# A linear-attention layer's products as 512 and 128 columns, keys one block ahead of values, and a closing stage that begins with two denominators

## The chip, the cores and the metric

The kernel runs on one core of one Trainium2 chip. The core has a matrix engine (TensorE, "PE"; its weight loads are listed apart as "PEld"), a vector engine (DVE), a scalar engine for activations (ACT), a general engine (POOL) and a queue engine (SP) that mostly issues transfers. Each engine runs its own list of instructions in order and waits on semaphores set by the others. The metric is the device time of the whole program in microseconds; the time of a kernel is the median of its runs.

## The reference

Two kinds of residual layer alternate, A, B, A, B, over 2048 tokens of width 640:

```
x = x + A(layernorm(x))     # twice, alternating with
x = x + B(layernorm(x))
```

A is attention with a recurrent memory: 64 segments of 32 tokens, each with 8 memory rows that are the first outputs of the segment before, 32 heads of 192. It is a chain of 64 dependent steps and takes most of the time. The change does not touch it. B is linear attention with a softmax feature map, 32 heads of 20:

```
q, k, v = split(x @ wqkv)                        # 32 heads x 20 each
pq, pk  = q @ w_phi[h], k @ w_phi[h]             # per head, 20 x 20
phi(p)  = [softmax(p), softmax(-p)]              # over the head's 20
kv      = sum over tokens of phi(pk)^T v         # per head, 40 x 20
z       = sum over tokens of phi(pk)
out     = (phi(pq) @ kv) / (phi(pq) @ z + 1e-6)
return out @ wo
```

No token's output can be formed before kv and z have been summed over all 2048 tokens, so the layer has two stages.

## The kernel before

The layers A run by a schedule that is written out by hand. A layer B is written as plain loops; a scheduler (Tile) orders its instructions on each engine by their dependences and by when buffers come free, so the order in the code is not always the order on the engine. The layers B run at about 1563 to 1863 us (layer 1) and 3420 to 3679 us (layer 3, the last). The end of the attention layer before it is computed inside B (`multiply`, lines 1192 to 1206): its products already go as 512 and 128 columns on one stationary block, into a kv bank and a side bank, and ACT and DVE evict them.

All products of B accumulate in PSUM, which has eight banks: three hold kv and z through the first stage (`kvp`), three rotate as the general banks (`bank()`, pool `pp`), two as the side banks (`side_bank()`, pool `ptp`). An instruction that wants a bank waits until the one that had it has been read out.

The layer works in four groups of 512 tokens, each of four blocks of 128. `norm_rows` adds the attention's output to the rows (POOL, line 360) and normalises them; `turn_rows` transposes them. The first stage of a group:

- `keys_values` (line 403), block by block. Keys (line 410): two halves of 320 columns, each of five matmuls over the input's 640 rows, into a bank each; ACT takes exp(p) and exp(-p) from each bank (line 413). DVE sums the exponentials of each head (line 416) and inverts the sums (line 418); POOL copies them beside the values (line 421). Values (line 425): again two halves; DVE multiplies each by the inverse sums (line 429). Then ten kv products of up to 126 columns (line 435). `w_phi` has been multiplied into the weights earlier (`fuse`).
- `query_norms` of the group before (line 451): the sums of the query exponentials (line 457), their logs on ACT (line 349), the difference on DVE (line 460), `split_exp` (lines 342 to 344: two exps on ACT, a subtraction on DVE), and then for six chunks of heads a spreading product (line 465) and a multiply on DVE (line 466).
- `queries` (line 446): six chunks of 120 (the last 40) rows by 512 tokens, with two exps each on ACT (line 449).

After the four groups kv and z are masked into block-diagonal form (`kvm`, `zm`, lines 512 to 520), and the closing stage runs: for a group, `denominators` (line 527: twelve matmuls of 512, then log and `split_exp`), `attention` (six chunks: two numerator matmuls, line 538, a spreading product of the inverse denominators, line 541, its copy on ACT, line 543, a multiply on DVE, line 544), and `output_rows` (per block two halves of 320 columns, line 555, the residual add on DVE, line 557, the store by POOL's queue, line 559; in layer 1 also the next layer's row norm and its store, line 563). The closing loop in full:

```
hl = denominators(0)
for g in range(NG):
    oT = attention(g, hl)
    if g + 1 < NG:
        hl = denominators(g + 1)
    if g == 0:
        query_norms(waiting)
    output_rows(g, oT)
```

So the first attention waits for one denominator, its log, two exponentials and a subtraction; later denominators are issued behind the attention before them. The norms of the last group (`waiting`) come behind the first attention. Denominators, norm sums and spreading products use the side banks.

Of the kernel before, what the change touches and what calls it, by code (L numbers as in the profile page):

```python
# [8 lines left out]
P = 128  # L9
# [106 lines left out]
class Kernel:  # L116
# [133 lines left out]
    def layer_B(self, x_dram, at_dram, xout_dram, xnext_dram, li, bp, post):  # L250
# [9 lines left out]
        HB2 = H // 2  # L260
        W2 = D // 2
# [13 lines left out]
        lgs, hls = self.views(take(4096), 2048, 2, F32), self.views(take(2048), 1024, 2)  # L275
# [19 lines left out]
        with tc.tile_pool(name=f"B{li}_kv", bufs=1, space=bass.MemoryType.PSUM, reuse_waits="tile") as kvp, \  # L295
                tc.tile_pool(name=f"B{li}_pt", bufs=2, space=bass.MemoryType.PSUM, reuse_waits="tile") as ptp, \
                tc.tile_pool(name=f"B{li}_ps", bufs=3, space=bass.MemoryType.PSUM, reuse_waits="tile") as pp:
# [104 lines left out]

            def keys_values(g, xnT):
                for b in range(4 * g, 4 * g + 4):
                    q = P * (b - 4 * g)
                    ek = eks.next().rearrange("p (s d) -> p s d", s=2)
                    for u in range(2):
                        ps = bank("ps_pk")
                        for k in range(KC):
                            nc.tensor.matmul(ps[:, 0:W2], lhsT=xnT[:, k, q:q + P],  # L410
                                             rhs=wqkv[:, k, D + W2 * u:D + W2 * u + W2], start=(k == 0), stop=(k == KC - 1))
                        for sg in range(2):
                            nc.scalar.activation(out=ek[:, sg, W2 * u:W2 * u + W2], in_=ps[:, 0:W2], func=ACT.Exp,
                                                 scale=1.0 - 2.0 * sg)
                    sk = bp.tile([P, 2 * H], F32, name="sk", tag="sk")
                    nc.vector.reduce_sum(out=sk[:], in_=ek[:, :, :].rearrange("p s (h f) -> p (s h) f", f=DH), axis=AX.X)
                    rk = bp.tile([P, 2, H], F32, name="rk", tag="rk")
                    nc.vector.reciprocal(out=rk[:, :, :].rearrange("p s h -> p (s h)"), in_=sk[:])

                    vr = vrs.next().rearrange("p (s h f) -> p s h f", s=2, h=H)  # L420
                    nc.gpsimd.tensor_copy(out=vr[:, :, :, DH], in_=rk[:])
                    for u in range(2):
                        ps = bank("ps_v")
                        for k in range(KC):
                            nc.tensor.matmul(ps[:, 0:W2], lhsT=xnT[:, k, q:q + P],
                                             rhs=wqkv[:, k, 2 * D + W2 * u:2 * D + W2 * u + W2], start=(k == 0),
                                             stop=(k == KC - 1))
                        for sg in range(2):
                            nc.vector.tensor_tensor(out=vr[:, sg, HB2 * u:HB2 * u + HB2, 0:DH],
                                                    in0=ps[:, 0:W2].rearrange("p (h f) -> p h f", f=DH),  # L430
                                                    in1=bcast_last(rk[:, sg, HB2 * u:HB2 * u + HB2], DH), op=ALU.mult)
                    for sg in range(2):
                        for c in range(NC_):
                            nh = sizes[c] // DH
                            nc.tensor.matmul(kv_out(sg, c), lhsT=ek[:, sg, CH * c:CH * c + sizes[c]],
                                             rhs=vr[:, sg, HC * c:HC * c + nh, :].rearrange("p h f -> p (h f)"),
                                             start=(b == 0 and (NC_ * sg + c) % 4 == 0), stop=(b == NB - 1),
                                             skip_group_check=True)

# [11 lines left out]
            def query_norms(g):  # L451
# [10 lines left out]
                for c in range(NC_):  # L462
                    mc = sizes[c]
                    pe = side_bank("ps_e")
# [28 lines left out]
            for g in range(NG):  # L493
# [10 lines left out]
                if waiting is not None:  # L504
                    query_norms(waiting)
# [16 lines left out]
            def denominators(g):  # L522
                tk = slice(512 * g, 512 * g + 512)
                ps = side_bank("ps_den")
# [6 lines left out]
            def attention(g, hl):  # L531
                tk = slice(512 * g, 512 * g + 512)
                oT = oTs.next().rearrange("p (c t) -> p c t", c=NC_)
                for c in range(NC_):
# [5 lines left out]
                    pe = side_bank("ps_e")  # L540
# [6 lines left out]
            def output_rows(g, oT):  # L547
                for b in range(4 * g, 4 * g + 4):
# [3 lines left out]
                    for u in range(2):  # L552
                        ps = bank("ps_wo")
                        for c in range(NC_):
                            nc.tensor.matmul(ps[:, 0:W2], lhsT=oT[0:sizes[c], c, q:q + P],
                                             rhs=wo[0:sizes[c], c, W2 * u:W2 * u + W2], start=(c == 0), stop=(c == NC_ - 1))
# [685 lines left out]
```

## Time and profile before

| | |
|---|---|
| time, median of 3 runs | 3674.0 us (3673.94 to 3683.37) |
| the profiled execution: its own time | 3680.76 us |
| the profiled execution: span | 3678.8 us |
| PE busy | 3527.4 us (96%) |
| DVE, ACT, POOL busy | 2339.3, 2044.9, 1653.2 us |
| granted clock, mean | 0.98 |
| a steady group of 512 tokens, layer 1 | 31.7 us |
| start of the closing stage, layer 1 and 3 | 24.6 and 21.5 us |
| the rest of it, layer 1 and 3 | 79.1 and 60.1 us |

The span runs from the first instruction to the last one of the profiled execution; its own time lies 2.0 us above it. "PEclk" is the clock that TensorE was granted, where 1.00 is full speed, and a matmul of the same shape takes twice as long at 0.50. A row of the timeline or of a group names the engine, the line of the kernel, the operation, and its tiles (output, then inputs, with partitions by elements); in brackets stands the idle time of the engine just ahead of it and what ended that.

### The profile page before, as it was taken

The numbers are of one execution on the slowest core, as the hardware profiler recorded it, in microseconds if no ns is written. First come the engines' busy times: TensorE is split into PE (matmuls) and PEld (weight loads), VectorE is DVE, ScalarE is ACT, GpSimd is POOL, SyncE is SP. The second block draws the span as 40 slices with busy tenths as digits, with TensorE's granted clock in tenths as the row PEclk, the third lists the DMA queues.
The fourth block names the chain that finished last, engine by engine and source line by source line (L and its number), as shares of the span: only waits on it lengthen the run. The fifth ranks groups of instructions, "written<-read, shape, count | busy, mean of one in ns | idle before, by whom it ended". The sixth has DMA issues, their size and how long they took to land.

```text
span 3678.8 us, 168780 instructions
## 1 busy us (share of the span) xinstructions
PE 3527.4 (96%) x70978; PEld 2301.1 (63%) x71271; DVE 2339.3 (64%) x6292; ACT 2044.9 (56%) x5233; POOL 1653.2 (45%) x4309
## 2 busy tenths in 40 slices
PE   9999999999999999999999899999999999999998
PEld 7766666666666666655367666666666666666553
DVE  5566666666666666556433566666666666666464
ACT  3356666666666656546332566666666666666462
POOL 3445555555555555430342455555555555555300
PEclk9999999999999999989799999999999999999998
DMA  8988888888888878840377887888888888888500
GB/s 296 342 296 293 277 279 292 285 277 294 283 274 291 290 266 289 304 140 1 135 255 203 292 286 273 292 290 279 295 283 278 289 288 274 289 293 299 155 1 29
DMA packets 531731, 933.33 MB, mean 254 GB/s; under 512 B 141066, under 2 KB 298394, under 8 KB 530970
## 3 DMA queue, kind: packets, MB, share of 16 engines
q1 hardware_dynamic: 428794, 818.87, 63.6%
q0 software_dynamic: 68512, 90.42, 8.3%
q10 hardware_dynamic: 33664, 13.24, 1.4%
q8 instruction: 557, 9.13, 1.0%
q14 instruction: 204, 1.67, 0.1%
HBM read 852.43 MB, written 73.73 MB: 252 GB/s over the span
## 4 chain that ended last, share of the span: by engine, by line
PE 37%; DMA 6%; DVE 4%; ACT 3%; issue 3%; PEld 2%; POOL 1%; SPq 0%; POOLq 0%; ACTq 0%; DVEq 0%
PE ps_qk L948 10%; PE ps_w L1024 4%; PE ps_v L948 4%; PE ps_o L998 2%; PE ps_s L990 2%; DMA arena<-wo_rows 2%; PE ps_pq L446 1%; PE ps_s L1056 1%; PEld L839 1%; DVE hT L904 1%; PE ps_s L985 1%; DMA kqb<-arena 1%; PE ps_idle L1031 1%; DMA arena<-in_A_Wv_dram 1%; PE ps_pk L410 1%
## 5 line engine op out<-in xcount | busy, mean ns | idle before, releaser
L948 PEld LDWEIGHTS <-hT 128*32 128x32 bf16 x30720 | 738.5, 96 | 433.5 <-DVE hT L1168 29.3
L948 PE MATMUL ps_qk<-arena,hT 128*32 128x384 bf16 x20480 | 996.9, 327 | 12.7 <-DMA arena<-in_A_Wk_dram 3.3
L958 ACT ACTIVATE raw<-ps_qk 128x384 bf16<-128x384 f32 x1024 | 503.1, 491 | 379.1 <-PE ps_s L1056 243.8
L1024 PE MATMUL ps_w<-arena,OT 128*32 128x160 bf16 x24576 | 540.9, 234 | 27.5 <-issue 14.9
L931 POOL DMA_DIRECT2D Vp<-vb x512 | 258.8, 505 | 653.9 <-PE ps_o L998 450.6
L948 PE MATMUL ps_v<-arena,hT 128*32 128x384 bf16 x10240 | 537.4, 330 | 5.6 <-DMA arena<-in_A_Wv_dram 5.5
L1024 PEld LDWEIGHTS <-OT 128*32 128x32 bf16 x24576 | 434.9, 97 | 120.3 <-issue 41.7
L963 DVE STREAM_TRANSPOSE KT<-raw 128x384 bf16<-128x384 bf16 x512 | 296.0, 578 | 196.6 <-ACT raw L958 192.6
L966 DVE STREAM_TRANSPOSE QT<-raw 128x256 bf16<-128x256 bf16 x512 | 227.9, 445 | 238.8 <-ACT raw L958 196.1
L919 POOL DMA_DIRECT2D kqb<-kqb x512 | 291.1, 569 | 174.6 <-POOL KT L927 147.9
L979 DVE CAST Vp<-ps_v 64x384 bf16<-64x384 f32 x512 | 286.0, 559 | 95.4 <-ACT Vp L977 80.5
L1017 POOL DMA_DIRECT2D otb<-otb x512 | 282.8, 552 | 110.1 <-DVE otb L1013 96.3
L977 ACT ACTIVATE Vp<-ps_v 64x384 bf16<-64x384 f32 x512 | 246.3, 481 | 150.7 <-PE ps_v L948 113.2
L1004 DVE CAST OT<-ps_o 128x192 bf16<-128x192 f32 x512 | 183.2, 358 | 214.8 <-PE ps_o L998 196.6
L1063 DVE TENSOR_TENSOR E<-E,ps_s 80x320 bf16<-80x320 bf16 x512 | 247.6, 484 | 73.7 <-ACT ps_s L1062 69.7
L1042 ACT ACTIVATE E<-ps_s 80x320 bf16<-80x320 f32 x512 | 221.9, 433 | 124.2 <-PE ps_s L990 95.7
L998 PEld LDWEIGHTS <-Vp 80*128 80x128 bf16 x4096 | 183.7, 99 | 159.4 <-issue 124.6
L998 PE MATMUL ps_o<-E,Vp 80*128 80x80 bf16 x4096 | 234.5, 202 | 24.4 <-DMA Vp<-vb 5.0
L990 PE MATMUL ps_s<-QT,KT 128*80 128x80 bf16 (+1 forms) x3072 | 233.6, 213 | 21.5 <-DVE KT L963 13.2
L1003 ACT ACTIVATE OT<-ps_o 128x192 bf16<-128x192 f32 x512 | 167.8, 328 | 147.6 <-PE ps_o L998 147.3
L912 ACT ACTIVATE Vp<-ps_w 32x160 bf16<-32x160 f32 x512 | 150.7, 294 | 167.4 <-DVE wt L1167 152.5
L990 PEld LDWEIGHTS <-KT 128*80 128x80 bf16 x3072 | 195.0, 119 | 70.7 <-issue 60.9
(157 smaller groups left out, 5329.9 us busy)
## 6 DMA issues: line engine op xcount, KB each, us to landing
arena<-wo_rows SPq DMA_DIRECT2D x792, 320.0 KB, 6.8
arena<-in_A_Wq_dram SPq DMA_DIRECT2D x427, 384.0 KB, 4.7
arena<-in_A_Wv_dram SPq DMA_DIRECT2D x427, 384.0 KB, 6.3
arena<-in_A_Wk_dram SPq DMA_DIRECT2D x768, 192.0 KB, 4.7
kqb<-kqb POOLq DMA_DIRECT2D x512, 48.0 KB, 5.1
arena<-in_A_Wk_dram SPq DMA_DIRECT2D x43, 384.0 KB, 7.1
vb<-arena POOLq DMA_DIRECT2D x128, 112.0 KB, 6.0
Vp<-vb POOLq DMA_DIRECT2D x512, 28.0 KB, 4.8
```

Source lines behind the costliest of these rows:

```text
L919: nc.gpsimd.dma_start(out=kqb[:], in_=self.kqb_d[s, :, r, :])
L931: nc.gpsimd.dma_start(out=Vs[n % 2][64:80, :], in_=self.vb_d[s, r].rearrange("g t f -> (g t) f"))
L948: nc.tensor.matmul(o[32 * g:32 * g + 32, 0:384], lhsT=hT[:, b, :], rhs=rhs, start=(i == 0), stop=(i == KC - 1), tile_position=(0, 32 * g), ...
L958: nc.scalar.activation(out=raw[:], in_=ps[:, 0:384], func=ACT.Copy)
L963: nc.vector.transpose(out=KT[:, :, 0:64], in_=raw[:, :].rearrange("p (c j) -> p c j", j=64))
L977: nc.scalar.activation(out=o, in_=i, func=ACT.Copy)
L979: nc.vector.tensor_copy(out=o, in_=i)
L990: nc.tensor.matmul(S[0:80, c0:c0 + 80 * (q1 - q0)], lhsT=KT[:, 3 * x + i, :], rhs=QT[:, x, q0:q1, :], start=False, stop=(x == 1 and i == 2 ...
L998: nc.tensor.matmul(O[x][:, 80 * i:80 * i + 80], lhsT=Vs[n % 2][0:80, 448 * x + k:448 * x + k + 128], rhs=E[0:80, 160 * x + 80 * e:160 * x ...
L1017: nc.gpsimd.dma_start(out=self.otb_d[s, :, 96 * r:96 * r + 96], in_=otb[:, :, :].rearrange("p c t -> p (c t)"))
L1024: nc.tensor.matmul(W[32 * g:32 * g + 32, 0:160], lhsT=OT[:, c, q:q + 32], rhs=w[:, 640 * i + 160 * g:640 * i + 160 * g + 160], start=(firs ...
L1063: nc.vector.tensor_tensor(out=E[0:80, 0:320], in0=E[0:80, 0:320], in1=rc, op=ALU.mult)
```

## The change

A helper, `pair`, issues for each of n input chunks a matmul of the first 512 columns and one of the last 128 on the same stationary block, into two general banks at once (500 and 140 for values, so that each part holds whole heads). Keys, values and output rows use it in place of two loops over halves of 320. ACT's exps and DVE's multiplies and adds are split in the same way. Keys of a block are issued before the values of the block before it. The banks are shared out as four general and one side bank. Norms and denominators are told which kind of bank to take; attention's spreading product takes a general one. The closing stage begins with the denominators of groups 0 and 1; the norms of the last group still follow the first attention, and each later group issues the denominator of the next. In the last layer the stores go by SP's queue.

```diff
-        lgs, hls = self.views(take(4096), 2048, 2, F32), self.views(take(2048), 1024, 2)
+        lgs, hls = self.views(take(4096), 2048, 2, F32), self.views(take(3072), 1024, 3)
...
-                tc.tile_pool(name=f"B{li}_pt", bufs=2, space=bass.MemoryType.PSUM, reuse_waits="tile") as ptp, \
-                tc.tile_pool(name=f"B{li}_ps", bufs=3, space=bass.MemoryType.PSUM, reuse_waits="tile") as pp:
+                tc.tile_pool(name=f"B{li}_pt", bufs=1, space=bass.MemoryType.PSUM, reuse_waits="tile") as ptp, \
+                tc.tile_pool(name=f"B{li}_ps", bufs=4, space=bass.MemoryType.PSUM, reuse_waits="tile") as pp:
...
+            def pair(name, split, n, lhsT, rhs):
+
+                ps = [bank(name) for _ in range(2)]
+                for k in range(n):
+                    for i, (lo, hi) in enumerate(((0, split), (split, D))):
+                        nc.tensor.matmul(ps[i][:, 0:hi - lo], lhsT=lhsT(k), rhs=rhs(k, lo, hi), start=(k == 0), stop=(k == n - 1))
+                return (ps[0], 0, split), (ps[1], split, D)
+
             def keys_values(g, xnT):
-                for b in range(4 * g, 4 * g + 4):
+                VS = DH * (512 // DH)
+
+                def tokens(b):
                     q = P * (b - 4 * g)
+                    return lambda k: xnT[:, k, q:q + P]
+
+                def keys(b):
                     ek = eks.next().rearrange("p (s d) -> p s d", s=2)
-                    for u in range(2):
-                        ps = bank("ps_pk")
-                        for k in range(KC):
-                            nc.tensor.matmul(ps[:, 0:W2], lhsT=xnT[:, k, q:q + P],
-                                             rhs=wqkv[:, k, D + W2 * u:D + W2 * u + W2], start=(k == 0), stop=(k == KC - 1))
+                    for ps, lo, hi in pair("ps_pk", 512, KC, tokens(b), lambda k, lo, hi: wqkv[:, k, D + lo:D + hi]):
                         for sg in range(2):
-                            nc.scalar.activation(out=ek[:, sg, W2 * u:W2 * u + W2], in_=ps[:, 0:W2], func=ACT.Exp,
-                                                 scale=1.0 - 2.0 * sg)
+                            nc.scalar.activation(out=ek[:, sg, lo:hi], in_=ps[:, 0:hi - lo], func=ACT.Exp, scale=1.0 - 2.0 * sg)
...
+                    return ek, rk
+
+                def values(b, ek, rk):
                     vr = vrs.next().rearrange("p (s h f) -> p s h f", s=2, h=H)
                     nc.gpsimd.tensor_copy(out=vr[:, :, :, DH], in_=rk[:])
-                    for u in range(2):
-                        ps = bank("ps_v")
...
+                    for ps, lo, hi in pair("ps_v", VS, KC, tokens(b), lambda k, lo, hi: wqkv[:, k, 2 * D + lo:2 * D + hi]):
+                        h = slice(lo // DH, hi // DH)
                         for sg in range(2):
-                            nc.vector.tensor_tensor(out=vr[:, sg, HB2 * u:HB2 * u + HB2, 0:DH],
-                                                    in0=ps[:, 0:W2].rearrange("p (h f) -> p h f", f=DH),
-                                                    in1=bcast_last(rk[:, sg, HB2 * u:HB2 * u + HB2], DH), op=ALU.mult)
+                            nc.vector.tensor_tensor(out=vr[:, sg, h, 0:DH],
+                                                    in0=ps[:, 0:hi - lo].rearrange("p (h f) -> p h f", f=DH),
+                                                    in1=bcast_last(rk[:, sg, h], DH), op=ALU.mult)
...
+                before = None
+                for b in range(4 * g, 4 * g + 4):
+                    now = (b, *keys(b))
+                    if before is not None:
+                        values(*before)
+                    before = now
+                values(*before)
...
-            def query_norms(g):
+            def query_norms(g, new):
...
-                    pe = side_bank("ps_e")
+                    pe = new("ps_e")
...
-                    query_norms(waiting)
+                    query_norms(waiting, side_bank)
...
-            def denominators(g):
+            def denominators(g, new):
...
-                ps = side_bank("ps_den")
+                ps = new("ps_den")
...
-                    pe = side_bank("ps_e")
+                    pe = bank("ps_e")
...
-                    for u in range(2):
-                        ps = bank("ps_wo")
-                        for c in range(NC_):
-                            nc.tensor.matmul(ps[:, 0:W2], lhsT=oT[0:sizes[c], c, q:q + P],
-                                             rhs=wo[0:sizes[c], c, W2 * u:W2 * u + W2], start=(c == 0), stop=(c == NC_ - 1))
-                        nc.vector.tensor_tensor(out=ob[:, W2 * u:W2 * u + W2], in0=ps[:, 0:W2], in1=x2[:, b, W2 * u:W2 * u + W2],
-                                                op=ALU.add)
-                    nc.gpsimd.dma_start(out=xout_dram[rows, :], in_=ob[:])
+                    for ps, lo, hi in pair("ps_wo", 512, NC_, lambda c: oT[0:sizes[c], c, q:q + P],
+                                           lambda c, lo, hi: wo[0:sizes[c], c, lo:hi]):
+                        nc.vector.tensor_tensor(out=ob[:, lo:hi], in0=ps[:, 0:hi - lo], in1=x2[:, b, lo:hi], op=ALU.add)
+                    (nc.sync if xnext_dram is None else nc.gpsimd).dma_start(out=xout_dram[rows, :], in_=ob[:])
...
-            hl = denominators(0)
+            hl = [denominators(0, side_bank), denominators(1, bank)]
             for g in range(NG):
-                oT = attention(g, hl)
-                if g + 1 < NG:
-                    hl = denominators(g + 1)
+                oT = attention(g, hl.pop(0))
                 if g == 0:
-                    query_norms(waiting)
+                    query_norms(waiting, bank)
+                elif g + 1 < NG:
+                    hl.append(denominators(g + 1, side_bank))
                 output_rows(g, oT)
```

More of the change, by code (lines that the diff above doesn't have):

```diff
@@ L259, in layer_B @@
         NG, NB = self.NG, self.NB
-        HB2 = H // 2
-        W2 = D // 2
         at = 0
@@ L418, in keys_values @@
                     nc.vector.reciprocal(out=rk[:, :, :].rearrange("p s h -> p (s h)"), in_=sk[:])
+                    return ek, rk
+                def values(b, ek, rk):
                     vr = vrs.next().rearrange("p (s h f) -> p s h f", s=2, h=H)
                     nc.gpsimd.tensor_copy(out=vr[:, :, :, DH], in_=rk[:])
-                    for u in range(2):
-                        ps = bank("ps_v")
[L424 to L427, printed above, removed]
+                    for ps, lo, hi in pair("ps_v", VS, KC, tokens(b), lambda k, lo, hi: wqkv[:, k, 2 * D + lo:2 * D + hi]):
+                        h = slice(lo // DH, hi // DH)
                         for sg in range(2):
-                            nc.vector.tensor_tensor(out=vr[:, sg, HB2 * u:HB2 * u + HB2, 0:DH],
-                                                    in0=ps[:, 0:W2].rearrange("p (h f) -> p h f", f=DH),
-                                                    in1=bcast_last(rk[:, sg, HB2 * u:HB2 * u + HB2], DH), op=ALU.mult)
+                            nc.vector.tensor_tensor(out=vr[:, sg, h, 0:DH],
+                                                    in0=ps[:, 0:hi - lo].rearrange("p (h f) -> p h f", f=DH),
+                                                    in1=bcast_last(rk[:, sg, h], DH), op=ALU.mult)
                     for sg in range(2):
```

## The prediction

> **What bounds the kernel now.** I read the page first, then the two linear layers stretch by stretch (busy time by windows), then TensorE's timeline inside them, then the releasers of its gaps. The page:
>
> ```profile
> span 3678.8 us, 168780 instructions
> PE 3527.4 (96%) x70978; PEld 2301.1 (63%) x71271; DVE 2339.3 (64%) x6292; ACT 2044.9 (56%) x5233; POOL 1653.2 (45%) x4309
> PEclk9999999999999999989799999999999999999998
> PE 37%; DMA 6%; DVE 4%; ACT 3%; issue 3%; PEld 2%; POOL 1%; SPq 0%; POOLq 0%; ACTq 0%; DVEq 0%
> ```
>
> TensorE is busy 96% of the span and no other engine comes near. The change touches only the linear layer, which runs near 1563–1863 and 3420–3679 us: 560 of 3679 us. There the granted clock dips. Windows of layer 1 (lines 1–2) and layer 3: length, PE, PEld, DVE, ACT and POOL busy, clock, DMA share, GB/s.
>
> ```profile
> 1690.50:1722.20 31.70, 29.59 (x198) 17.96 (x198) 20.78 (x37) 20.22 (x43) 2.50 (x5) 1.00 0.00 1
> 1753.60:1778.20 24.60, 22.09 (x55) 6.67 (x54) 5.86 (x14) 8.91 (x16) 0.00 (x0) 0.67 0.69 258
> 3462.90:3492.60 29.70, 24.57 (x160) 15.79 (x158) 18.87 (x40) 11.70 (x27) 11.68 (x21) 0.94 0.15 44
> 3587.50:3609.00 21.50, 19.10 (x56) 6.14 (x54) 5.89 (x14) 8.79 (x16) 0.00 (x0) 0.76 0.00 1
> 3609.00:3669.10 60.10, 59.63 (x277) 25.26 (x276) 33.68 (x60) 15.95 (x27) 8.15 (x15) 0.94 0.11 40
> ```
>
> A steady group of 512 tokens (line 1) takes 31.7 us at full clock with 2.1 us idle; the start of closing (lines 2, 4) has 55 matmuls that last 19–22 us because the clock is 0.67–0.76. TensorE's timeline (start, us, ..., [idle before <-releaser]):
>
> ```profile
> 1569.80 0.38 PE L1198 MATMUL kv<-arena 128*128 128x512 bf16 x1
> 1570.02 0.22 PE L1199 MATMUL ps_post<-arena 128*128 128x128 bf16 x1
> 1570.07 0.38 PE L1198 MATMUL kv<-arena 128*128 128x512 bf16 x1
> ...
> 1661.63 1.53 PE L410 MATMUL ps_pk<-arena 128*128 128x320 bf16 x10
> 1663.00 1.52 PE L425 MATMUL ps_v<-arena 128*128 128x320 bf16 x10
> ...
> 1703.97 0.84 PE L410 MATMUL ps_pk<-arena 128*128 128x320 bf16 x5 [1.08 <-ACT arena L413]
> ...
> 3474.68 0.27 PE L435 MATMUL kv<-arena 128*120 128x126 bf16 x2 [1.72 <-POOL arena L421]
> ...
> 3594.59 0.59 PE L541 MATMUL ps_e<-arena 64*120 64x512 bf16 x2 [1.93 <-DVE arena L344]
> 3595.65 1.07 PE L541 MATMUL ps_e<-arena 64*120 64x512 bf16 x2 [0.47 <-ACT arena L543]
> ...
> 3627.80 3.12 PE L527 MATMUL ps_den<-arena 120*64 120x512 bf16 x12
> ...
> 3647.34 8.26 PE L555 MATMUL ps_wo<-arena 120*128 120x320 bf16 x48
> ```
>
> See four things. A 512+128 pair already exists in the attention tail: start to start 0.27 us. Keys stall on the exponentials that read their banks. Closing stands 1.93 us for one denominator's Ln, two exps and subtraction, then runs ten microseconds at half clock. The 48 output products take 8.26 us, not 48 x 0.137 = 6.6.
>
> **Pairs (keys, values, output).** 512 pairs take the place of 1024 matmuls of 320 columns: 2 layers x 16 blocks x (5 + 5 + 6). Row: ten 320s in 1.37 us (1661.63 to 1663.00) are 0.274 for two; the tail's pair is 0.271. So nothing. [...] The weight loads are not fewer here: each matmul still has its own. [...] In the trace the pair's 128 takes 0.05, its load hidden under the neighbouring 512, so I take 0; the range keeps +5.
>
> Output gains: six 320s take 1.02, not 0.82; the 0.2 is the chunk of 40 rows, visited twice per block before and once per block in pairs. 16 x 0.2 = 3.2 per layer. ACT and DVE sums do not move: an exp of 320 issues every 0.34, of 512 every 0.50, so 2 x 0.50 + 2 x 0.18 = 4 x 0.34; products 0.40 against 0.59 and 0.21 on 500/140.
>
> **Keys ahead of values.** In the compiled order a steady group becomes keys 0, keys 1, values 0, keys 2, values 1 with the kv products of block 0, and so on; banks are four instead of three, the side bank is one. Before, stalls are 1.23 or 1.08, 0.57 and 0.65 per group, so 31.7 - 2.4 = 29.3 is the floor. The new order removes the wait for ACT, since while keys' banks drain, values have others. It adds one: the value pair holds two of four banks until DVE has done reduce 0 (1.48), reduce 1 (1.48), reciprocals, and four products, and reduce 1 now stands ahead of products 0 on DVE. Behind it on TensorE stand the next values and all that follows. My walk with these durations gives 1.1 us before values 1 in groups 2 and 3, 1.2–1.9 in group 1. Gains per layer 0.7 + 1.3 + 1.3. The six ps_e of a group's norms, on one side bank instead of two, move beside the query products; their cover is 30 query matmuls (0.22 each), without which each is 0.6.
>
> The first group: in layer 3 POOL (four adds of 1.36 each before the first rk copy, 5.44 us) held kv by 1.72 and the clock fell; in layer 1 it starts at half clock. After, two adds still precede the first copy, but keys 1 cover them. Walk: a 2.3 us wait before values 1, total 24.4. Layer 3: 29.7 to 25.5, gain 4; layer 1: gain 1.5. Key stages: 5.5 + 2 x 3.3 = 12.1; I take 2 off per layer because a 2.3 us wait may cost the clock: 8.1.
>
> [...] The trace: idle of 1.23 left the clock at 1.00, 0.85+1.72 and 1.93+0.47 took it to half for about 8–11 us. [...]
>
> **Attention's tail.** It ends inside the linear layer and uses the side bank, of which one is left: the second tail block's ps_post must wait for the first one's eviction on ACT (1570.05 to 1570.33 before), some 1.2 us after that block starts at 1569.1. The compiled order puts seven 512s of 0.216 ahead, 1.5 us: cost 0; if the cover is gone, 0.3 of eviction for each of three blocks, bound +1.
>
> **Closing's start.** Two denominators are issued before the first attention, and their logs and exps overlap 12 more matmuls (3.05 at full clock; 3.12 in line 3627.80). Full-clock work is 3 x 3.05 (two denominators, sums of the norms as two halves of 1.5) + 5.25 of attention = 14.4. But the compiled order puts group 1's denominator ahead of group 0's, because the side bank is still busy with norms; so group 0's chain (Ln 0.59, exps 0.63 + 0.63, subtract 0.68; 2.6 us with hand-overs) is covered only by six sums of 1.5, leaving about 1.1 us of wait, under the 1.23 that left the clock alone. 14.4 + 1.1 + 2.1 for three norm products moved in and for waits on banks = 17.6, at full clock. Gain 24.6 - 17.6 = 7.0 and 21.5 - 17.6 = 3.9: 10.9.
>
> **Rest of closing.** Layer 3: outputs -0.9 per group; attention's ps_e now shares four banks with ps_num instead of 3 + 2, so a chunk is paced at 1.13 by ACT's copy and DVE's multiply instead of 0.93, +1.2 in each of three groups, partly filled by denominators. Walk 56.1 against 60.1: gain 4.0. Layer 1 is paced by POOL in the row norm (1.88 per centring, 3.5 per block), which pairs do not shorten; gain 2.9. ACT's e copies there now stand behind scales that wait on POOL; that is in the walk.
>
> **Stores.** Sixteen last-layer stores leave POOL's queue for SP's, which has nothing left but its loads, all done. End: POOL needs 0.54 to issue and 2.1 to land, SP's row of the same 160 KB is 2.7 to landing; the last add is now a 128, 0.4 later in the pair. -0.4, bounds -1.5 to +1.
>
> Sum 8.1 + 10.9 + 4.0 + 2.9 - 0.4 = 25.5. The profiled execution took 3680.8 (span 3678.8 + 2.0 around it), 6.8 above the median of 3674.0. 3680.8 - 25.5 = 3655.3; on the median 3648.5. A difference of 0.3% (11 us) is what a measurement here can tell.
>
> **The rivals.** Waits only change banks (0.16): value banks wait where key banks did, and key stages give nothing. For: DVE is busy 20.8 of 31.7 us and the reduces stand first. Against: the keys' banks no longer wait, and a walk that leaves a gain. The 8.1 is gone and the first group's wait costs 5 more at half clock: gain 12 to 13, 3661.
>
> The order undoes the point (0.14): group 0's denominator comes second, its chain uncovered, the clock still falls at closing, so the change doesn't do what it says. For: the compiled order. Against: the norms' sums still lie between. Loses 9: 3657.
>
> Both (0.08): 25.5 - 12.1 - 9 = 4.4, 3670.
>
> Slower (0.10): the new waits before values 1 take the clock down in every group. Place: both layers' eight groups, between the first and second values. Decides from somewhere between 1.23 (no drop) and 1.72 (drop). Price: 7–11 us at half clock lose 3.5–5.5 each; 8 x 4.5 = 36, less the gains of closing and stores (17.4) and of the six later groups (6.6): +12, 3686. For: waits of 1.2–1.9 in group 1 and 2.3 in group 0. Against: 1.1 in groups 2 and 3, where 1.23 cost nothing before.
>
> **How the numbers follow.** The forecast itself has 0.52. Range 3634 to 3672: the low end adds the clock allowance (4), 6 us of half clock that I left in layer 1's closing, and 4 for the looseness of the walk; the high end takes in all but the slower case. Faster by over 0.3% needs under 3663: the forecast, most of the first two rivals, 0.77; same 0.13, slower 0.10.
>
> **What would show it.** After: no 1.08 idle before keys on ACT; a new PE wait before the second values, released by DVE's product; clock 1.00 through the first closing window and its length about 17.6; denominators in 3.05 there; 24 output pairs in 7.3; group windows of 30.3–31; a chunk of attention at 1.13. Wrong if the clock falls inside a steady group, if the pair lasts over 0.29, or if the idle before the first ps_e of closing still is near 1.9.

## The result, and the profile after

The changed kernel took 3646.3 us in the median of six runs (3638.6 to 3660.3), the kernel before 3679.2 beside it. The ratio is 0.9912, 95% interval 0.9888 to 0.9937: 32 us faster, where 25.5 were forecast. The profiled execution took 3639.2 us against 3680.8.

The page of the changed kernel:

```profile
span 3637.2 us, 168714 instructions
PE 3499.8 (96%) x70946; PEld 2276.4 (63%) x71271; DVE 2334.2 (64%) x6292; ACT 2039.5 (56%) x5233; POOL 1639.7 (45%) x4293
PEclk9999999999999999999899999999999999999999
```

TensorE is still the engine that bounds the kernel. Its busy time fell by 28 us for as many matmuls (71271 weight loads in both), and one of the two dips of its clock is gone: layer 3 now has a clock of 1.00 from its second group to its last output product, where the kernel before had 0.50 for 10.24 us from 3595.09 and for 6.83 us from 3618.98. The windows of the changed kernel (length, PE, PEld, DVE, ACT and POOL busy, clock, DMA share, GB/s): a steady group and the start of closing in layer 1, then layer 3's first group, start of closing and rest of it.

```profile
1674.75:1704.80 30.05, 29.92 (x196) 15.92 (x196) 20.29 (x38) 19.53 (x42) 2.02 (x5) 1.00 0.01 1
...
1735.20:1759.60 24.40, 22.57 (x82) 7.91 (x80) 12.55 (x29) 12.52 (x21) 0.00 (x0) 1.00 0.72 259
...
3441.50:3469.70 28.20, 23.67 (x158) 14.24 (x158) 19.34 (x43) 11.63 (x31) 11.26 (x22) 0.94 0.16 47
...
3559.80:3584.40 24.60, 22.77 (x83) 7.95 (x82) 12.75 (x30) 12.52 (x21) 0.00 (x0) 1.00 0.00 1
3584.40:3633.00 48.60, 48.22 (x254) 19.54 (x253) 28.01 (x52) 12.26 (x21) 0.00 (x0) 1.00 0.13 48
```

The steady group has 30.05 us with 0.13 idle, where it had 31.7 with 2.1. Both starts of closing have a clock of 1.00, where it was 0.67 and 0.76. They look no shorter than before, but they now hold 82 matmuls instead of 55: a third denominator, 5 of the 12 products of the fourth and nine spreading products of the norms have moved ahead of the first output product. So closing has to be compared whole.

TensorE's timeline of the changed kernel (start, us, line, tiles, [idle before <-releaser]):

```profile
3397.71 0.55 PE L1207 MATMUL ps_post<-arena 128*128 128x128 bf16 x7 [1.28 <-ACT obB L1210]
...
3448.30 0.64 PE L406 MATMUL ps_v<-arena 128*128 128x500 bf16 x3 [1.12 <-ACT arena L420]
3451.36 0.58 PE L439 MATMUL kv<-arena 128*120 128x126 bf16 x4 [2.42 <-POOL arena L429]
...
3564.89 3.12 PE L539 MATMUL ps_den<-arena 120*64 120x512 bf16 x12
3568.69 1.57 PE L469 MATMUL ps_sq<-arena 120*64 120x512 bf16 x6 [0.68 <-ACT arena L347]
3570.72 0.37 PE L553 MATMUL ps_e<-arena 64*120 64x512 bf16 x1 [0.47 <-DVE arena L342]
...
3578.23 3.10 PE L539 MATMUL ps_den<-arena 120*64 120x512 bf16 x12 [0.68 <-ACT arena L347]
...
3584.36 7.42 PE L406 MATMUL ps_wo<-arena 120*128 120x512 bf16 x48
```

What is left to wait for is seen in these rows: the attention's tail waits for the only side bank (1.28), the first group for ACT and for POOL's copy (1.12 and 2.42), closing three times: twice for a log that holds the side bank (0.68 and 0.68) and once for the exponentials' subtraction (0.47). The 48 output products take 7.42 us instead of 8.26.

The two traces were cut at the same matmuls in both. This is where the 41.6 us between the two profiled executions lie, each number being a difference of two start times of matmuls:

| stretch | before | after | difference |
|---|---|---|---|
| unchanged work: start to layer 1's attention tail, and layer 2 | 3103.0 | 3096.5 | -6.5 |
| attention tail and weight fusion, both layers | 133.7 | 133.5 | -0.2 |
| first group, layer 1 / 3 | 27.5 / 29.4 | 25.3 / 28.1 | -2.2 / -1.3 |
| groups 1 to 3, each layer | 94.9 | 90.1 | -4.8 twice |
| closing, last query product to last output product, layer 1 | 103.7 | 96.0 | -7.6 |
| the same, layer 3 | 81.5 | 73.2 | -8.3 |
| last output product to the end | 10.05 | 4.23 | -5.8 |

The first row is not the change's: the attention layers run the same instructions in both kernels, and their times scatter whatever the kernel (in the thirteen traces, start to layer 1's tail took 1545 to 1567 us, layer 2 took 1547 to 1563). Without it the changed stretches give -35.1, near the 32 of the runs' ratio. Because whole runs scatter by ten microseconds and more, the experiments below are read by these stretches, and their ratios to the kernel before are given beside them.

### The profile page after: what moved, and what is told of

Same layout as the page of the kernel before. It is cut to its first block, busy times and chain, and to the rows that moved or that the text cites. A ratio compares the mean times of both kernels' runs of the same rounds, so it can differ in the third digit from the quotient of the medians.

```text
span 3637.2 us, 168714 instructions
## 1 busy us (share of the span) xinstructions
PE 3499.8 (96%) x70946; PEld 2276.4 (63%) x71271; DVE 2334.2 (64%) x6292; ACT 2039.5 (56%) x5233; POOL 1639.7 (45%) x4293
## 4 chain that ended last, share of the span: by engine, by line
PE 68%; DMA 11%; DVE 8%; ACT 5%; issue 4%; POOL 2%; PEld 2%; SPq 0%; POOLq 0%; DVEq 0%; ACTq 0%
PE ps_qk L956 20%; PE ps_w L1032 9%; PE ps_v L956 8%; DMA arena<-wo_rows 5%; PE ps_o L1006 5%; PE ps_s L998 4%; PE ps_pre L847 3%; PE ps_s L1064 3%; DVE hT L912 3%; PE ps_s L993 2%; PE ps_idle L1039 2%; ACT raw L966 2%; DVE E L1071 2%; PE ps_pre L871 2%; PE ps_pq L458 1%
## 5 line engine op out<-in xcount | busy, mean ns | idle before, releaser
L956 PE MATMUL ps_qk<-arena,hT 128*32 128x384 bf16 x20480 | 996.0, 327 | 12.1 <-DMA arena<-in_A_Wq_dram 1.9
L998 PE MATMUL ps_s<-QT,KT 128*80 128x80 bf16 (+1 forms) x3072 | 233.3, 213 | 22.2 <-DVE KT L971 12.9
L932 POOL COPY QT<-kqb 128x64 bf16<-128x64 bf16 x512 | 125.6, 245 | 253.1 <-PE ps_s L998 245.3
```

Source lines behind the costliest of these rows:

```text
L956: nc.tensor.matmul(o[32 * g:32 * g + 32, 0:384], lhsT=hT[:, b, :], rhs=rhs, start=(i == 0), stop=(i == KC - 1), tile_position=(0, 32 * g), ...
L998: nc.tensor.matmul(S[0:80, c0:c0 + 80 * (q1 - q0)], lhsT=KT[:, 3 * x + i, :], rhs=QT[:, x, q0:q1, :], start=False, stop=(x == 1 and i == 2 ...
```

## The experiments

**The end of the program.** The last store had left POOL's queue for SP's. Two kernels move that alone, one way and the other.

```diff
-                    (nc.sync if xnext_dram is None else nc.gpsimd).dma_start(out=xout_dram[rows, :], in_=ob[:])
+                    nc.gpsimd.dma_start(out=xout_dram[rows, :], in_=ob[:])
```

> The changed kernel, its last layer's stores on POOL's queue again. Theory (the queue's end, not the landing, sets the last stretch): the time from the last output product's start to the end goes from 4.2 us back to about 10.1, as before the change; the rest of layer 3 stays within 0.5; the whole is 5.5 to 6.5 slower than the changed kernel. Rival (the prediction's term: only issue and landing count, 0.54 + 2.1 against 2.7): 4.2 goes to 4.6, 0.4 slower.

```diff
-                    nc.gpsimd.dma_start(out=xout_dram[rows, :], in_=ob[:])
+                    (nc.sync if xnext_dram is None else nc.gpsimd).dma_start(out=xout_dram[rows, :], in_=ob[:])
```

> The kernel before, only its last layer's stores moved to SP's queue. Theory (queue's end): last output product to end 10.05 us goes to about 4.2, all else as before, 5.8 faster. Rival (landing alone): 9.6 to 10, no more than 0.4 faster.

Measured: 4.23 went back to 10.30 in the first, and 10.05 went to 3.97 in the second. The choice of queue for the last stores is worth 6 us by itself. The ratios are 0.9948 (0.9933 to 0.9962) for the first and 0.9986 (0.9970 to 1.0002) for the second, which is 5 us, with an interval that just takes in no gain. The first lost 13 against the changed kernel's ratio, more than 6; in its profiled execution the clock also fell to 0.50 in layer 3's closing (below), though the instructions there are the changed kernel's own. How much of the rest that is over all its runs was not measured.

What holds the end is seen in the closing lines of the kernel before: its last store, and the instructions of the program's end (line 1237, with durations min/median/max in ns).

```profile
3669.87 0.54 POOL L559 DMA_DIRECT2D out_dram<-arena  x1 [1.51 <-DVE arena L557]
```

```profile
L1237 POOLq DRAIN  x3: 46/102/8154, 3669.9 to 3678.5; - x3
L1237 SPq DRAIN  x3: 7/7/7, 3672.3 to 3678.3; - x3
```

The store was issued at 3669.87 and its data had landed by 3671.9, but a drain of POOL that began with it lasted 8.15 us, to 3678.0, 0.8 us before the end of the span. In the changed kernel the last store is SP's, landed 1.8 us after its issue, and the program ends 3.1 us after it:

```profile
3634.10 0.33 SPq L567 DMA_DIRECT2D out_dram<-arena  x1
```

```profile
L1245 POOLq DRAIN  x3: 46/106/6775, 3547.7 to 3636.9; - x3
```

POOL's long drain is not gone there: it takes 6.78 us, but it starts at 3547.7, with POOL's own last work, and is over 82.7 us before the end. In the two kernels whose last store is POOL's the end took 10.05 and 10.30 us, in the two where it is SP's 4.23 and 3.97: the 6 us come with POOL's last instruction being the program's last.

**What shortened the groups.** The change does three things there: keys ahead, pairs, and a fourth general bank. A group is measured here from the last query product of one group to that of the next. One kernel takes away the first, one the second, and one has the third alone.

```diff
-                before = None
                 for b in range(4 * g, 4 * g + 4):
-                    now = (b, *keys(b))
-                    if before is not None:
-                        values(*before)
-                    before = now
-                values(*before)
+                    values(b, *keys(b))
```

> The changed kernel, each block's values again straight behind its own keys; pairs, four general banks and one side bank stay. Theory (keys ahead take the waits out of a group): a steady group goes from 30.0 us back to 31.3 to 32, with idle ahead of keys or of kv products that ends on ACT or DVE; both layers' key stages together 10 to 14 slower. Rival (the fourth general bank takes them out): the group stays at 29.7 to 30.4 and the whole within 3 of the changed kernel.

```diff
-                    for ps, lo, hi in pair("ps_pk", 512, KC, tokens(b), lambda k, lo, hi: wqkv[:, k, D + lo:D + hi]):
+                    for ps, lo, hi in halves("ps_pk", KC, tokens(b), lambda k, lo, hi: wqkv[:, k, D + lo:D + hi]):
...
-                    for ps, lo, hi in pair("ps_v", VS, KC, tokens(b), lambda k, lo, hi: wqkv[:, k, 2 * D + lo:2 * D + hi]):
+                    for ps, lo, hi in halves("ps_v", KC, tokens(b), lambda k, lo, hi: wqkv[:, k, 2 * D + lo:2 * D + hi]):
```

> The changed kernel, keys and values as two separate passes of 320 columns again; keys ahead, banks, closing and output pairs stay. Theory (a pair costs as much as two halves): steady group 29.8 to 30.4, the whole within 3 of the changed kernel. [...]

```diff
-                tc.tile_pool(name=f"B{li}_pt", bufs=2, space=bass.MemoryType.PSUM, reuse_waits="tile") as ptp, \
-                tc.tile_pool(name=f"B{li}_ps", bufs=3, space=bass.MemoryType.PSUM, reuse_waits="tile") as pp:
+                tc.tile_pool(name=f"B{li}_pt", bufs=1, space=bass.MemoryType.PSUM, reuse_waits="tile") as ptp, \
+                tc.tile_pool(name=f"B{li}_ps", bufs=4, space=bass.MemoryType.PSUM, reuse_waits="tile") as pp:
```

> The kernel before, only its banks shared out as four general and one side bank. Theory (the fourth general bank takes the waits out of a group, whatever the order and the split): groups 1 to 3 together go from 94.9 us to 89 to 91 in each layer; the closing stage, whose spreading products now share one side bank, gets longer. Rival (the bank helps only together with keys ahead or with pairs): 93.5 to 95.

| kernel | groups 1, 2, 3 | sum, each layer | closing, layer 1 / 3 | ratio to before |
|---|---|---|---|---|
| before | 31.74, 31.68, 31.52 | 94.9 | 103.7 / 81.5 | 1 |
| changed | 29.74, 29.99, 30.41 | 90.1 | 96.0 / 73.2 | 0.9912 (0.9888 to 0.9937) |
| without keys ahead | 29.25, 30.93, 30.05 | 90.2 | 104.6 / 80.3 | 0.9966 (0.9955 to 0.9978) |
| without pairs in keys and values | 28.54, 30.38, 30.20 | 89.1 | 104.7 / 73.8 | 0.9909 (0.9885 to 0.9934) |
| before, with four and one banks | 29.31, 29.17, 29.91 | 88.4 | 113.2 / 99.5 | 1.0018 (1.0002 to 1.0033) |

In these groups the fourth general bank does all of it. With it alone they are 6.5 us shorter per layer, shorter than in the changed kernel; taking keys ahead away changes their sum by 0.1, and two separate halves are 1.0 per layer quicker than the pairs. The window of group 2 with four banks and nothing else has no idle at all:

```profile
1681.23:1710.39 29.16, 29.16 (x196) 17.56 (x195) 20.53 (x37) 19.88 (x42) 2.07 (x5) 1.00 0.01 1
```

In the first group the halves are quicker still: 22.2 us in layer 1 and 25.8 in layer 3, where the pairs take 25.3 (1 us of it by a clock of 0.50 in its first 2 us) and 28.1. The waits of the values for ACT, 1.12 and 0.89 with pairs in layer 3, are 0.17 and 0.16 there, and the wait for POOL stays:

```profile
3478.02 0.84 PE L414 MATMUL ps_v<-arena 128*128 128x320 bf16 x5 [0.17 <-ACT arena L429]
3480.87 0.27 PE L448 MATMUL kv<-arena 128*120 128x126 bf16 x2 [2.01 <-POOL arena L438]
...
3485.74 0.43 PE L414 MATMUL ps_v<-arena 128*128 128x320 bf16 x2 [0.16 <-ACT arena L429]
```

So for keys and values the pairs lose, most of it in the first group. The whole kernel's ratio does not show it: its closing in layer 1 took 104.7 us where the changed kernel's took 96.0, and the mean clock of its profiled execution was 0.984 against 0.987.

But the bank is taken from somewhere. With one side bank and spreading products that still go there, closing took 99.5 instead of 81.5 us in layer 3 and 113.2 instead of 103.7 in layer 1, and the kernel as a whole was not faster. Its timeline there:

```profile
3586.95 4.69 PE L527 MATMUL ps_den<-arena 120*64 120x512 bf16 x12 [0.77 <-DVE arena L466]
...
3594.35 0.58 PE L541 MATMUL ps_e<-arena 64*120 64x512 bf16 x1 [2.72 <-DVE arena L344]
3595.61 0.58 PE L541 MATMUL ps_e<-arena 64*120 64x512 bf16 x1 [0.69 <-ACT arena L543]
```

The denominator waits for DVE to free the side bank from the norms (0.77), its own chain then stands uncovered (2.72), and a spreading product waits for the copy that frees the bank from the one before (0.69). The kernel with one denominator first (below) has four and one banks too, but its spreading products take general banks, and it closes in 76.8 us in layer 3, of which the output pairs explain some 3. So the move of the spreading products to the general banks, which looks like a detail of the diff, is the likely reason why the fourth bank pays; no run moved it alone. The kernel without keys ahead loses its 7 to 9 us per layer in closing, where its idle is spread otherwise (one wait of 1.46 in each layer); the mean clock of its profiled execution was 0.982 against 0.987. Why the order of keys and values changes the idle there has not been taken apart.

**Two denominators first.**

```diff
-            hl = denominators(0)
+            hl = [denominators(0, side_bank), denominators(1, bank)]
             for g in range(NG):
-                oT = attention(g, hl)
-                if g + 1 < NG:
-                    hl = denominators(g + 1)
+                oT = attention(g, hl.pop(0))
                 if g == 0:
                     query_norms(waiting)
+                elif g + 1 < NG:
+                    hl.append(denominators(g + 1, side_bank))
```

> The kernel before, only its closing stage begun with two denominators (the second in a general bank) and the third denominator moved behind the second attention. Halves of 320, three general and two side banks as before. Theory (cover of group 0's chain keeps the clock): the two denominators take 6.1 us in a row at full clock, the idle ahead of the first spreading product is below 1 us, clock 1.00 to the first output product; layer 3's closing from last query product to last output product goes from 81.5 to 73 to 77, layer 1's from 103.7 to 97 to 101, the whole 8 to 13 faster. Rival (the norms, whose sums wait for side banks and logs, let the clock fall anyway): closing 81.5 goes to 79 to 82, the whole within 4.

In the kernel before, that alone took closing from 103.7 to 93.9 and from 81.5 to 71.5 us, 20 together; the ratio is 0.9959 (0.9944 to 0.9974). Its timeline in layer 3 has no wait between the last query product and the output:

```profile
3585.43 6.16 PE L527 MATMUL ps_den<-arena 120*64 120x512 bf16 x24
3591.52 0.86 PE L538 MATMUL ps_num<-arena 120*120 120x512 bf16 x3
3592.31 0.42 PE L541 MATMUL ps_e<-arena 64*120 64x512 bf16 x1
```

The two denominators stand in a row, so group 1's covers the chain of group 0's. Layer 3's closing is 1.7 us shorter than the changed kernel's own, although its output products are still halves. The opposite experiment, the changed kernel with one denominator first, was meant to be its mirror:

```diff
-            hl = [denominators(0, side_bank), denominators(1, bank)]
+            hl = [denominators(0, side_bank)]
...
+                if g + 1 < NG:
+                    hl.append(denominators(g + 1, side_bank))
                 if g == 0:
                     query_norms(waiting, bank)
-                elif g + 1 < NG:
-                    hl.append(denominators(g + 1, side_bank))
```

> The changed kernel with the closing stage begun as before: one denominator, then attention, the next denominator behind it, the last group's norms after. Theory (one group's chain of log, exps and subtraction uncovered takes the clock down): an idle of 1.9 us or more on TensorE ahead of the first spreading product, then half clock for some 10 us; layer 3's closing (last query product to last output product) 73.2 goes to 79 to 83, layer 1's 96.0 to 100 or more; the whole 8 to 14 slower. Rival (closing's gain is in the output pairs and the banks, the clock's fall came from something else): idle of about 2, no fall of the clock, closing 2 us longer in each layer, the whole 3 to 5 slower.

It does not decide: closing grew by 2.7 and 3.6 us, the ratio is 0.9939 (0.9922 to 0.9956). With one side bank the scheduler put the last spreading products of the norms ahead of the first denominator, the idle came in pieces of 0.7 to 0.8, and the clock had a mean of 0.94 over 29.0 us there in layer 3 (as much as one step of 3.4 us at 0.50 takes off) and of 1.00 over 25.0 us in layer 1. Neither theory had this.

**The output products.** Here the halves stay, and only the order of chunks is turned round in the second one.

```diff
-                        for c in range(NC_):
+                        order = range(NC_) if u == 0 else range(NC_ - 1, -1, -1)
+                        for i, c in enumerate(order):
```

> The kernel before, the second half of each output block run through its chunks backwards, so that the 40-row chunk's two products stand next to each other and are entered once a block instead of twice. Theory (0.2 us each time the rows of the stationary block change): 48 output products of 320 go from 8.26 to 7.3 to 7.6 us, layer 3's rest of closing is 3 faster, the whole 4 to 6. Rival (what shortened them in the changed kernel is the pair itself, 512 and 128 on one stationary block): 8.1 to 8.3, the whole unchanged.

```profile
3644.52 7.53 PE L556 MATMUL ps_wo<-arena 120*128 120x320 bf16 x48
```

7.53 us against 8.26 and the pairs' 7.42: nearly all of the pairs' gain in the output rows is that the chunk of 40 rows is entered once per block. The ratio is 0.9984 (0.9969 to 1.0000), 6 us. In layer 3 closing went from 81.5 to 75.2, about 3 of it by the products and the rest by the 6.83 us at a clock of 0.50 that the kernel before has from 3618.98 and this trace has not. Layer 1 gained nothing (closing 105.6); the last kernel below shows what POOL does there.

**The first group of layer 3.**

```diff
-                    nc.gpsimd.tensor_copy(out=vr[:, :, :, DH], in_=rk[:])
+                    (nc.vector if g == 0 else nc.gpsimd).tensor_copy(out=vr[:, :, :, DH], in_=rk[:])
```

> The changed kernel, the first group's four copies of the inverse sums on DVE instead of POOL. Theory (in layer 3 POOL's queue of residual adds holds the first kv product): the 2.42 us idle that ends on POOL's copy is gone, layer 3's first group goes from 28.1 to 25 to 26, layer 1's stays at 25.3; the whole 2 to 3 faster. Rival (another wait is due at the same time: the products on DVE, or the banks of the second values): the idle ends on DVE or ACT instead and the group gains less than 1.

The group went from 28.13 to 25.20 us in layer 3, and the wait on POOL was gone (with the same first stage and POOL's copies it took 28.1 to 30.1 in three traces, with DVE's 24.3 to 25.2 in three):

```profile
3466.11 0.39 PE L439 MATMUL kv<-arena 128*120 128x126 bf16 x4 [0.16 <-DVE arena L433]
```

The ratio is 0.9888 (0.9867 to 0.9910). Layer 1's group was 24.4; in the two later kernels with the same copies it was 25.6 and 25.7, so nothing was gained there.

**A version from these.** The kv banks are free in closing. The next kernel keeps the copies on DVE and puts there the denominators and one norm sum; the one after it also subtracts layer 1's row means on DVE.

```diff
-            hl = [denominators(0, side_bank), denominators(1, bank)]
+            def kv_bank(j):
+                return lambda name: kv_ps[j]
+
+            hl = [denominators(0, kv_bank(0)), denominators(1, kv_bank(1))]
...
-                    query_norms(waiting, bank)
+                    query_norms(waiting, bank, (side_bank, kv_bank(2)))
                 elif g + 1 < NG:
-                    hl.append(denominators(g + 1, side_bank))
+                    hl.append(denominators(g + 1, kv_bank(g - 1)))
```

> The changed kernel with the first group's copies on DVE, and with the closing stage's denominators and one of the norm sums in the kv banks, which nothing uses any more by then. Theory (the closing waits of 0.68, 0.47 and 0.68 come from the one side bank, and the clock falls when over 1.1 us of them lie within one 3.4 us step): group 0's denominator comes first, its chain is covered by group 1's, no idle over 0.3 to the first output product, clock 1.00 there in both layers; last query product to first output product 24.6 goes to 22 to 23. Rival (another wait, on the general banks or on the norms' logs, takes their place): idle stays over 1 us, 24 or more.

```diff
-                        self.ln_rows(bp, ob, xn, centre=nc.gpsimd, scale=nc.scalar)
+                        self.ln_rows(bp, ob, xn, scale=nc.scalar)
```

> The kernel of after_kv_sums, and in layer 1's closing the rows' mean is subtracted on DVE instead of POOL. Theory (POOL's 1.88 us a block paces that stage): first to last output product of layer 1 goes from 71.5 to 52 to 60, the granted clock there to 0.95 or more, the whole 12 to 20 faster than after_kv_sums; layer 3 as there. Rival (DVE, whose adds, statistics and products already fill half of it, or ACT's scales become the pace): 64 to 70, 2 to 7 faster.

Windows of the second one: start of closing and rest of it in layer 1, then start of closing in layer 3.

```profile
1758.20:1781.50 23.30, 23.30 (x85) 7.79 (x83) 12.75 (x30) 12.40 (x21) 0.00 (x0) 1.00 0.74 271
1781.50:1843.30 61.80, 55.01 (x251) 21.48 (x250) 46.89 (x124) 27.29 (x60) 21.29 (x57) 0.86 0.33 107
3571.30:3594.50 23.20, 23.20 (x85) 7.78 (x83) 12.65 (x30) 12.40 (x21) 0.00 (x0) 1.00 0.00 1
```

TensorE has no idle at all in either start of closing. The stretch came to 23.3, above the 22 to 23 that was expected. Closing went to 94.1 and 70.4 with the banks (96.0 and 73.2 in the changed kernel) and to 85.1 and 70.4 with DVE too. Layer 1's rest of closing is 61.8 against 71.5; it was expected at 52 to 60, and TensorE still stands idle for 6.8 of it, at a clock of 0.86, with DVE busy 46.9 of 61.8. The ratios are 0.9907 (0.9888 to 0.9925) and 0.9873 (0.9849 to 0.9896). The last is the fastest kernel of the study by its ratio; its interval overlaps the changed kernel's, so its lead rests on the stretches. The first one's gain does not show in its ratio, which is no better than that of the kernel with DVE's copies alone.

## Why the prediction was right, point by point

**Direction, size and cause.** Faster by 25.5 was forecast, 32 (by the ratio) came. The terms of the sum came out unequally: against the stretches of the profile, groups gave 5.0 more than the 8.1 they stood at, closing 1.9 less, the stores 6.2 more. That the sum is near is in part luck: the largest surprise, the stores, was not foreseen at all, and the groups' gain came from another cause than the one worked out.

**Groups.** Predicted 12.1, or 8.1 with the allowance for the clock; measured 13.1. The size is right, the account is not. The step "adds one: the value pair holds two of four banks" foresaw a wait of 1.1 to 1.9 before the second values in groups 1 to 3, released by DVE; there is none. The one wait in these groups is 0.42 before the third values of group 3, and it ends on ACT:

```profile
1719.38 0.37 PE L406 MATMUL ps_v<-arena 128*128 128x500 bf16 x1 [0.42 <-ACT arena L420]
```

Idle is down to 0.1 to 0.5 in each of the three. The working gave the gain to the order. The runs give it to the bank, which the prediction named in half a sentence. In the first group of layer 3 the step "two adds still precede the first copy, but keys 1 cover them" failed: the wait on POOL grew from 1.72 to 2.42, and the gain was 1.3 instead of 4. The rival that the waits only change banks was right for the first group: the 1.12 before its second values is the keys' old wait for ACT. The half clock after 0.85+1.72 was read too long, too: before the change it lasted one step of 3.4 us there, and 10.2 and 17.1 at the two starts of closing, not about 8 to 11. And the 1.23 that was called harmless stands in no row: it is 1703.97 less 1702.05 less five products of 0.137; the row has 1.08, the longest wait of groups 1 to 3 before the change.

**Closing.** 17.8 was predicted in two layers (10.9 + 4.0 + 2.9), 15.9 came. The order, group 1's denominator ahead of group 0's, was there, and the wait of "about 1.1 us" that it leaves was 0.68 + 0.47. That the wait would leave the clock alone held in this profile, where it stayed at 1.00, by luck: in the kernel with stores on POOL the same waits were followed by 0.50 (last section). The stretch of 17.6 was set against the wrong content, since 17 more products of denominators and nine of the norms had moved into it; it took 24.6. Attention's pace was over-charged: 1.13 per chunk was predicted, and the chain that ended last has 0.93, as before:

```profile
3622.21 0.57 PE ps_num L550 x2
3622.78 0.35 PE ps_e L553
3623.14 0.57 PE ps_num L550 x2
3623.71 0.35 PE ps_e L553
3624.06 0.57 PE ps_num L550 x2
```

**Pairs.** The trace said 0 (0.271 for a pair, 0.274 for two halves), and the range kept 5 for them; no run shows that figure. The runs show 1.0 per layer in groups 1 to 3, for 120 pairs, 0.008 each. Order and waits differ between those two kernels as well, so 1.0 is an upper bound only if nothing else offsets it. What pairs cost in the first group, 3.1 and 2.3 us with their waits, the working did not look for. Output products were predicted at 7.3 and took 7.42, from the cause given.

**Stores.** This is the term that was mis-sized: in the sum it stands as a loss of 0.4, and a gain of 5.8 came, 6.1 by itself, outside the bounds of -1.5 and +1. The working took the time to landing as what ends the program. Between the end of the last issue and the end of the span stood 8.4 us, of which landing explains 1.5; what filled them was POOL's drain of 8.15.

**Attention's tail.** Cost 0 was taken because seven 512s cover the eviction. They do not quite: the wait was 1.28 in layer 3 here, and 0.40 to 1.28 in nine places of five other kernels with the one side bank; in the other three it was 0.23 or nothing. The stretch as a whole changed by 0.2.

## What to carry to other kernels

Before crediting a new order of loops, ask what the same diff does to the number of buffers, and run that alone: here a bank was worth the whole gain of the groups, and cost up to 18 us a layer where it had been taken from. Look at what the engine that issues the last transfer still has to do after it, and not only at when the data land. Waits that one profile shows free are worth removing: here the same 0.68 and 0.47 came with a clock of 1.00 and a closing of 73.2 us in one execution, with 0.50 and 85.0 in another.

## What the runs showed of the hardware that had not been expected

In the traces of the kernel before and of the changed kernel the granted clock is 1.00 or 0.50 in every stretch, and neighbouring changes of it (37 and 27 in number) lie whole multiples of 3.41333 us apart, to within 0.003. At the starts of closing, how much of one such step TensorE stood idle went with the clock of the next step. Two executions of the same instructions show it. The first pair of windows is the kernel with stores on POOL, the second the changed kernel, each one step and the step after it.

```profile
3585.02:3588.43 3.41, 2.26 (x9) 0.95 (x9) 0.68 (x1) 2.34 (x4) 0.00 (x0) 0.99 0.00 0
3588.43:3591.84 3.41, 3.41 (x7) 0.70 (x5) 1.38 (x2) 1.18 (x3) 0.00 (x0) 0.50 0.00 0
```

```profile
3567.25:3570.66 3.41, 2.33 (x9) 0.87 (x8) 0.67 (x1) 1.85 (x3) 0.00 (x0) 1.00 0.00 0
3570.66:3574.07 3.41, 3.35 (x11) 1.02 (x10) 1.40 (x3) 2.09 (x4) 0.00 (x0) 1.00 0.00 0
```

The waits of 0.68 and 0.47 both fell into one step in the first (3.41 - 2.26 = 1.15 idle), and the clock halved for 27 us and closing took 85.0 us; in the second the grid cut them (1.08 idle), and it took 73.2. The kernel before has a step with 2.40 us of idle at the start of closing in layer 1 (from 1758.72) and one with 1.93 in layer 3 (from 3591.68), and each was followed by 0.50. In the changed kernel no step there had more than the 1.08, and the clock stayed at 1.00 in both layers.

Idle time does not sort the steps of the whole program. In the groups of the first stage, in these two traces, a step with 1.12 kept the clock (changed kernel, from 1625.03), and 1.91 and 2.77 lost it (3472.21 before, 3447.74 after). In the rest of closing, with its products of 40 and 64 rows, a step with 0.42 lost it (before, from 3615.57) and one with 1.07 kept it (after, from 1788.87). So idle time alone is not the measure; what else counts, no run here shows. The prediction had carried the first stage's reading (1.23, in the rows 1.08, harmless and 1.72 costly) over to closing, and had taken it as a property of one gap, where in the windows above two gaps in one step, 0.68 and 0.47, went before 0.50. The same gaps went either way in these two executions; how much of the scatter between runs that makes was not measured.
